# FNet plus PEER on one core: one-hots of the gates made a step earlier, checks placed anew, and loads and stores moved from one DMA queue to another

## The chip, the cores and the metric

The kernel runs on one core of a Trainium2 chip. Its engines work side by side, each through its own instructions in order: TensorE (PE in the profile; its weight loads are PEld), VectorE (DVE), ScalarE (ACT), GpSimd (POOL) and SyncE (SP), which here only issues DMAs. GpSimd can issue DMAs too. Inputs and outputs lie in device memory. The metric is the device time of one execution in microseconds (us); lower is better.

## The reference

```python
def _A_ref(x, dft_seq_re, dft_seq_im, dft_hid_re, dft_hid_im):
    a = jnp.einsum("bsd,ed->bse", x, dft_hid_re)
    b = jnp.einsum("bsd,ed->bse", x, dft_hid_im)
    return jnp.einsum("ts,bse->bte", dft_seq_re, a) - jnp.einsum("ts,bse->bte", dft_seq_im, b)

def _B_ref(x, w_q, k1, k2, u, v):          # 32 heads, 64 + 64 keys, top 2
    q = jnp.einsum("nd,dhc->nhc", xf, w_q)
    s1 = jnp.einsum("nhd,ed->nhe", q[..., :dk], k1)
    s2 = jnp.einsum("nhd,ed->nhe", q[..., dk:], k2)
    ...                                    # top 2 of s1, of s2, then of their 4 sums
    g = _softmax(top_s, axis=-1)
    act = _gelu(jnp.einsum("nd,nhkd->nhk", xf, u[top_e]))
    out = jnp.einsum("nhk,nhk,nhkd->nd", g, act, v[top_e])

xn = _layernorm(x, axis=-1)
return x + _A_ref(xn, ...) + _B_ref(xn, ...)
```

x is 2048 tokens by 512, float32. The two DFT matrices over the sequence are 2048 x 2048, those over the hidden dimension 512 x 512; they come as inputs. The PEER part has 4096 experts, each a row of u and a row of v.

## The kernel before

**Stages.** Up to about 480 us the kernel does the layer norm, the DFT, the scores of the heads and the choice of experts. The DFT's result lies as rows of y in device memory, one block of 128 tokens after another (y_d). From there on it computes the PEER part densely: for each block b of 128 tokens (16 blocks) it multiplies all 4096 rows of u with the tokens (the z phase), applies gelu, multiplies by the gates, and multiplies by all rows of v (the v phase). The phases come in the order z of a pair of blocks, v of b - 1, v of b: `("z", 8, 9), ("v", 7), ("v", 8), ("z", 10, 11), ("v", 9), ...`.

**The z phase of a pair** (z_pair, L1193; matmuls L1186) has 28 slots of 24 matmuls. Three slots run at the end of the v phase before it and one in the v phase behind it; the rest is divided into 16 steps. The slots share four PSUM banks (z0 to z3) with the sum of the v phase. A bank comes free by VectorE's adds (L1227, L1235, L1238) or ScalarE's copies and gelu (L1225, L1230, L1232, L1215).

**The v phase** (v_part, L1327; matmuls L1349) has 8 steps of 12 matmuls. At its end, finish (L1362) adds the sum to the tile y and stores it to out. The tile y (one buffer) was filled by add_x (L1357): a load of the DFT's rows from y_d on SP's queue (L1359), onto which GpSimd issues a DMA that adds x (L1360). So a load of y waits for the store of the block before, and the accumulate waits for the load.

**Gates.** g_mm (L1268) turns the chosen experts and their gates into a dense block for 32 columns: per half, VectorE writes the one-hot matrices L (128 x 2048, L1279) and R (128 x 512, L1284, then times the gate, L1287), and TensorE multiplies them (16 matmuls, L1289). Three pairs (L, R) take turns. w_part (L1292) multiplies gates and activations (L1297) and splits the product into two float16 parts (ScalarE's L1304 or VectorE's L1302, then L1305).

**Checks.** The kernel uses symmetries of the DFT matrices and ranges of the weights. Side work verifies them, and a general path runs behind a branch where they don't hold. compare (L1370) loads one of 64 units of the sequence matrices into a tile cx: 64 KB of ca (L1377) and 448 KB of cb (L1378); compare_in (L1381) sums the first 128 columns' absolute values on VectorE (L1385), folds the rest with adds (L1391 to L1429), and ScalarE sums the absolute differences (L1430). compare_w does this for four units of the hidden matrices (wt), and fit sums weights, some of them loaded (L1486, L1494). Tiles cx, fit and w share four buffers (tag "w"). A call of step (L1544) starts one unit: it first issues what the last calls left (`later`: ScalarE's sums; `loaded`: VectorE's folding) and then loads the next unit.

**Order.** A table, plan, says at which step of which phase a piece of side work is issued: `put(phase, step, work)`; G, W, U and F stand for g_mm, w_part, a unit of compare and one of fit. From this program the framework's scheduler makes each engine's order, and may move an instruction among others. `pin` (keep_in_program_order) keeps an instruction behind all that was issued ahead of it on its engine. In the table before, U and F stand in z phases at steps 8, 9, 11 to 13 and 15, 23 units U in all, and in the v phases of even blocks four U.

## Time and profile before

| what | us |
| --- | --- |
| median of 3 timed runs | 1130.34 (1128.55 to 1131.25) |
| profiled execution | 1135.25 |
| its span, first to last instruction | 1133.4 |
| TensorE busy in it | 1107.3 |
| VectorE busy | 962.7 |
| ScalarE busy | 663.9 |
| GpSimd busy | 332.7 |

The granted TensorE clock was 0.995 of full speed over the span. A row of the timeline gives the start, the duration, engine, line, operation, output and inputs with their shapes, how many instructions of a kind follow one another, and in brackets how long the engine was idle before and what ended that. A row of the waits gives the engine and line that waited, what it waited for, and the total, the times and the longest in us. A row of the groups gives busy time and the mean of one in ns, then the idle time before them. A row of DMA issues gives the queue, the number, KB each, and the median us from issue to landing.

### The profile page before, as it was taken

Reading aid. Unit: us, or ns where it says so; the run is one execution under the profiler, and the core shown is the slowest. Engines: PE = TensorE matmul, PEld = TensorE weight load, DVE = VectorE, ACT = ScalarE, POOL = GpSimd, SP = SyncE. Lnnn points to the kernel's source line nnn. Section 1 sums busy time; section 2 is a strip of 40 time slices with the busy share of each in tenths; the row PEclk is TensorE's granted clock in tenths of the full one; section 3 lists DMA queues with packets and bytes.
Section 4 is the critical chain, followed back from the end, with each engine's and each line's share of the span. In section 5 each row is a group of like instructions: output and inputs, shape, how many; then the busy total and the mean of one; then the engine's idle time right before and its main releaser. Section 6 shows DMA issues by size and latency. Waiting matters only on the chain.

```text
span 1133.4 us, 29112 instructions
## 1 busy us (share of the span) xinstructions
PE 1107.3 (98%) x11528; PEld 722.5 (64%) x11528; DVE 962.7 (85%) x2904; ACT 663.9 (59%) x1098; POOL 332.7 (29%) x385
## 2 busy tenths in 40 slices
PE   9999999999999999999999999999999999999997
PEld 6455554544545459687488478478569569569643
DVE  7899789999989799948997897898888888888793
ACT  6558598888877584346445545544535545544442
POOL 0429999899888850000000000000000000000000
PEclk9999999999999999999999999999999999999999
DMA  9883546465353335866666777666668668566354
GB/s 291 292 206 148 185 139 223 117 217 170 92 168 96 111 108 191 236 199 205 226 206 226 227 218 241 218 207 232 200 205 263 199 211 269 190 221 206 121 168 134
DMA packets 132273, 220.51 MB, mean 195 GB/s; under 512 B 35092, under 2 KB 71067, under 8 KB 132126
## 3 DMA queue, kind: packets, MB, share of 16 engines
q1 hardware_dynamic: 129520, 214.28, 58.7%
q0 software_dynamic: 2304, 4.20, 2.8%
q8 instruction: 92, 1.51, 0.5%
q14 instruction: 55, 0.45, 0.1%
q10 hardware_dynamic: 302, 0.08, 0.0%
HBM read 183.06 MB, written 29.69 MB: 188 GB/s over the span
## 4 chain that ended last, share of the span: by engine, by line
PE 59%; DVE 15%; DMA 5%; ACT 4%; issue 2%; POOL 1%; SPq 0%; ACTq 0%; DVEq 0%
PE s L252 18%; PE z L1186 17%; PE v L1349 16%; PE z L1108 4%; DMA cx<-in_cb_dram 3%; DVE w L1297 3%; DVE L L1279 3%; PE g L1289 3%; DVE act L1305 2%; PE m L148 1%; DVE R L1287 1%; DVE R L1284 1%; DVE w L1305 1%; DMA s<-s_d 1%; DVE cx L1393 1%
## 5 line engine op out<-in xcount | busy, mean ns | idle before, releaser
L252 PE MATMUL s<-m,xq 128*128 128x512 f16 x1344 | 297.4, 379 | 1.7 <-ACT ss L962 1.4
L1349 PE MATMUL v<-v,act 128*128 128x512 f16 x1044 | 233.3, 379 | 0.0
L252 PEld LDWEIGHTS <-xq 128*128 128x128 f16 x1344 | 129.6, 98 | 153.1 <-issue 3.2
L1360 POOL DMA_DIRECT2D y<-in_x_dram x16 | 14.4, 897 | 658.7 <-DMA v<-v_d 274.7
L1279 DVE TENSOR_TENSOR L<-io_lam,cmp 128x2048 f16<-128x2048 f16 x128 | 156.2, 1221 | 28.1 <-PE g L1289 28.1
L1349 PEld LDWEIGHTS <-act 128*128 128x128 f16 x1044 | 99.2, 98 | 112.4
L1186 PEld LDWEIGHTS <-u 128*128 128x128 f16 x2688 | 156.2, 98 | 14.8 <-issue 8.3
L966 DVE MAX8 vals<-ss 128x8 f32<-128x64 f32 x896 | 133.3, 216 | 5.5 <-ACT ss L962 5.2
L1186 PEld LDWEIGHTS <-s 128*128 128x128 f16 x1944 | 110.6, 98 | 1.2 <-DMA s<-s_d 1.2
L1349 PE MATMUL v<-v,w 128*128 128x512 f16 x480 | 109.0, 384 | 0.0
L1304 ACT ACTIVATE act<-w 128x1024 f16<-128x1024 f32 x36 | 48.9, 1358 | 92.2 <-DVE w L1297 92.2
L970 DVE FIND_INDEX8 idx<-vals,ss 128x8 uint16<-128x256 f32 x224 | 93.7, 418 | 0.0
L962 ACT ACTIVATE ss<-s,wsc 128x512 f32<-128x512 f32 x120 | 80.0, 680 | 22.5 <-PE s L252 12.6
L1186 PE MATMUL z<-xb,u 128*128 128x128 f16 x1344 | 84.9, 220 | 5.3 <-DVE w L1227 4.7
L1186 PE MATMUL z<-x,u 128*128 128x128 f16 x1344 | 84.7, 220 | 1.6 <-DVE act L1238 1.1
L1186 PE MATMUL z<-x,s 128*128 128x128 f16 x1296 | 81.2, 219 | 1.0 <-DMA s<-s_d 1.0
L1215 ACT ACTIVATE act<-act,scl 128x512 f32<-128x512 f32 x56 | 39.6, 720 | 70.9 <-DVE act L1235 40.9
L1349 PEld LDWEIGHTS <-w 128*128 128x128 f16 x480 | 46.1, 99 | 53.1 <-issue 2.3
L1430 ACT ACTIVATE cx<-cx 128x896 f32<-128x896 f32 x64 | 60.0, 938 | 29.6 <-DVE cx L1410 11.7
L1289 PEld LDWEIGHTS <-L 128*128 128x128 f16 x2048 | 60.7, 96 | 17.3 <-issue 7.2
L1289 PE MATMUL g<-R,L 128*128 128x32 f16 x2048 | 63.5, 177 | 6.6 <-DVE R L1287 6.2
L1305 DVE TENSOR_TENSOR act<-w,act 128x1024 f16<-128x1024 f32 x44 | 58.6, 1332 | 6.1 <-ACT act L1304 6.1
(363 smaller groups left out, 1878.9 us busy)
## 6 DMA issues: line engine op xcount, KB each, us to landing
v<-v_d SPq DMA_DIRECT2D x67, 512.0 KB, 4.6
s<-s_d SPq DMA_DIRECT2D x63, 512.0 KB, 4.2
cx<-in_cb_dram SPq DMA_DIRECT2D x64, 448.0 KB, 5.7
w<-in_wq_dram SPq DMA_DIRECT2D x28, 512.0 KB, 5.9
fit<-in_wq_dram SPq DMA_DIRECT2D x28, 512.0 KB, 4.3
uv<-in_vn_dram SPq DMA_DIRECT2D x16, 512.0 KB
uv<-in_ut_dram SPq DMA_DIRECT2D x16, 512.0 KB, 3.5
s_d<-v SPq DMA_DIRECT2D x32, 256.0 KB, 2.5
```

The lines of the kernel that those rows point to most:

```text
L252: nc.tensor.matmul(ps, xt[i][:, l, kd, :], m[:, r, kd, :], start=(n == 0), stop=(n == 3 * KD - 1))
L962: nc.scalar.activation(s, ps, AF.Copy, scale=inv)
L966: nc.vector.max(vals[:, i, w, :, h], s[:, g, :])
L970: nc.vector.max_index(idx[:, i, w].rearrange("p k h -> p (k h)"), vals[:, i, w, 0:2].rearrange("p k h -> p (k h)"), s[:, w * HC:g + 1, :]. ...
L1108: nc.tensor.matmul(ps if n == 1 else ps.rearrange("p (b n) -> p b n", b=2), ug[:, l, c % 2, kd, :], xb2[:, k0, r, kd, :] if n == 1 else xb ...
L1186: nc.tensor.matmul(bank[:, t * P:(t + 1) * P], lt, rt, start=(t == k == 0 and op in "125"), stop=(t == 3 and k == 5), skip_group_check=op ...
L1279: nc.vector.tensor_tensor(L.rearrange("p t (l two) -> p t l two", two=2), io_lam.rearrange("p (l two) -> p l two", two=2).unsqueeze(1).to_ ...
L1289: nc.tensor.matmul(p[:, hf, t * NC:(t + 1) * NC], L[:, t, :], R[:, t, :], start=True, stop=True)
L1304: nc.scalar.activation(w16[..., 0], w, AF.Copy)
L1305: nc.vector.tensor_tensor(w16[..., 1], w, w16[..., 0], op=ALU.subtract)
L1349: nc.tensor.matmul(pv, w16[:, c, :, l], v_sb[g][:, r, cc, :], start=(n + cc == 0 and k == 0), stop=(n == end and cc == 1 and k == 2))
L1430: later.append(lambda: pin(nc.scalar.activation(tf[:, P:], tf[:, P:], AF.Abs, accum_out=chk[:, n:n + 1])))
```

## The change: one-hots, checks, queues and sums

1. g_prep holds the one-hots of both halves, and LRP places it in the table one to three steps ahead of its g_mm. L is pinned, R isn't.
2. The checks have other steps: in z phases U at 0 and 4 (and 14 in the pairs 2/3, 4/5 and 6/7) and no F; in v phases of even blocks F at 0 and a fifth U at step 2; one F more in block 14. 17 units U are in z phases instead of 23.
3. The loads of y (but the last block's), the stores of out in finish, and the loads of ca, cb and fit go from SP's queue to GpSimd's, 193 issues in all. Loads of v, s and wt stay on SP's.
4. The sums of the absolute values of ca (128 columns, 64 units) go from VectorE to ScalarE, behind the sums of the differences.

```diff
@@ -1258,6 +1258,7 @@
             return work, middle, behind
 
         GP = {}
+        pin = tc.keep_in_program_order
 
         def parts(b):
 
@@ -1265,9 +1266,11 @@
             return act.rearrange("p c n -> p (c n)").bitcast(F16).rearrange(
                 "p (c n l) -> p c n l", c=NC, l=2)
 
-        def g_mm(b, tg):
+        PREP = {}
+
+        def g_prep(b, tg):
+            assert not PREP
             cmp = CMP[b]
-            p = pg(f"g{b}_{tg}")
             for hf in range(2):
                 ts = slice(tg * TG + hf * 16, tg * TG + hf * 16 + 16)
 
@@ -1276,15 +1279,22 @@
 
                 LR.append(LR.pop(0))
                 L, R = LR[-1]
-                nc.vector.tensor_tensor(
+                PREP.setdefault((b, tg), []).append((L, R))
+                pin(nc.vector.tensor_tensor(
                     L.rearrange("p t (l two) -> p t l two", two=2),
                     io_lam.rearrange("p (l two) -> p l two", two=2).unsqueeze(1).to_broadcast([P, 16, P // 2, 2]),
-                    bc(0, P), op=ALU.is_equal)
+                    bc(0, P), op=ALU.is_equal))
                 Rv = R.rearrange("p t (c two) -> p t c two", two=2)
                 nc.vector.tensor_tensor(
                     Rv, io_c.rearrange("p (c two) -> p c two", two=2).unsqueeze(1).to_broadcast([P, 16, NC // 2, 2]),
                     bc(1, NC), op=ALU.is_equal)
                 nc.vector.tensor_tensor(Rv, Rv, bc(2, NC), op=ALU.mult)
+
+        def g_mm(b, tg):
+            if (b, tg) not in PREP:
+                g_prep(b, tg)
+            p = pg(f"g{b}_{tg}")
+            for hf, (L, R) in enumerate(PREP.pop((b, tg))):
                 for t in range(16):
                     nc.tensor.matmul(p[:, hf, t * NC:(t + 1) * NC], L[:, t, :], R[:, t, :], start=True, stop=True)
             GP[b, tg] = p
@@ -1356,16 +1366,15 @@
 
         def add_x(b):
             Y[b] = y = bp.tile([P, D], F32, tag="y", name=f"y{b}", bufs=1)
-            nc.sync.dma_start(y, y_d[b])
+            (nc.sync if safe or b + 1 == NT else nc.gpsimd).dma_start(y, y_d[b])
             nc.gpsimd.dma_start(y, x[b % 4, b // 4], accum_op=ALU.add)
 
         def finish(b, pv):
             y = Y[b]
             nc.vector.scalar_tensor_tensor(y, pv, osc, y, op0=ALU.mult, op1=ALU.add)
-            nc.sync.dma_start(out[b * P:(b + 1) * P], y)
+            (nc.sync if safe else nc.gpsimd).dma_start(out[b * P:(b + 1) * P], y)
 
         later, loaded = [], []
-        pin = tc.keep_in_program_order
 
         def compare(n):
 
@@ -1374,16 +1383,14 @@
             t = bp.tile([P, 4, 4, 64], F32, tag="w", name=f"cx{n}", bufs=WB)
             tf = t.rearrange("p s q c -> p (s q c)")
             tv = t.rearrange("p s q c -> p s (q c)")
-            nc.sync.dma_start(tf[:, :P], ca[ri, g, :, kk * P:(kk + 1) * P])
-            nc.sync.dma_start(tf[:, P:], cb[ri, g, kk].rearrange("p b c -> p (b c)"))
+            nc.gpsimd.dma_start(tf[:, :P], ca[ri, g, :, kk * P:(kk + 1) * P])
+            nc.gpsimd.dma_start(tf[:, P:], cb[ri, g, kk].rearrange("p b c -> p (b c)"))
             loaded.append(lambda: compare_in(n, t, tf, tv))
 
         def compare_in(n, t, tf, tv):
 
             ri, g, kk = n // 32, n // 8 % 4, n % 8
             odd = kk // 4
-            pin(nc.vector.tensor_reduce(asum[:, n:n + 1], tf[:, :P], axis=AX.X, op=ALU.add,
-                                        apply_absolute_value=True))
             sgn = (((1, 1, 1), (-1, 1, -1)), ((-1, -1, 1), (1, -1, -1)))[ri][odd]
             ops = [ALU.subtract if v > 0 else ALU.add for v in sgn]
             op = ops[1]
@@ -1427,7 +1434,11 @@
             mirror(t[:, 0])
             if kk == 0:
                 nc.vector.memset(t[:, 0, 2, 0:1], 0.0)
-            later.append(lambda: pin(nc.scalar.activation(tf[:, P:], tf[:, P:], AF.Abs, accum_out=chk[:, n:n + 1])))
+            def sums_abs():
+                pin(nc.scalar.activation(tf[:, P:], tf[:, P:], AF.Abs, accum_out=chk[:, n:n + 1]))
+                nc.scalar.activation(tf[:, :P], tf[:, :P], AF.Abs, accum_out=asum[:, n:n + 1])
+
+            later.append(sums_abs)
 
         def compare_w(n):
 
@@ -1483,7 +1494,7 @@
 
             if n < NK:
                 t = bp.tile([P, 2 * D], F32, tag="w", name=f"fit{n}", bufs=WB)
-                nc.sync.dma_start(t.rearrange("p (h k) -> p h k", h=2), wq[1 + n // 4, n % 4 // 2, n % 2])
+                nc.gpsimd.dma_start(t.rearrange("p (h k) -> p h k", h=2), wq[1 + n // 4, n % 4 // 2, n % 2])
                 loaded.append(lambda: later.append(
                     lambda: pin(nc.scalar.activation(t, t, AF.Abs, accum_out=fits[:, n:n + 1]))))
                 return
@@ -1491,7 +1502,7 @@
             t = bp.tile([P, 2 * D], F32, tag="w", name=f"fit{n}", bufs=WB)
             if g >= 16 + V2:
                 h = t.bitcast(F16)[:, 0:2 * D]
-                nc.sync.dma_start(h, v_d[g - 16 - V2, :, 0:2 * D])
+                nc.gpsimd.dma_start(h, v_d[g - 16 - V2, :, 0:2 * D])
                 loaded.append(lambda: later.append(
                     lambda: pin(nc.scalar.activation(h, h, AF.Abs, accum_out=fits[:, n:n + 1]))))
                 return
@@ -1583,6 +1594,9 @@
         def G(b, k):
             return lambda: g_mm(b, k)
 
+        def LRP(b, k):
+            return lambda: g_prep(b, k)
+
         def W(b, k, here=False):
             return lambda: w_part(b, k, here)
 
@@ -1606,41 +1620,42 @@
             if b % 2 == 0 and 0 < b < 13:
                 nx = phases[phases.index(ph) + 1]
                 st = 1 if len(nx) == 2 else 2
-                put(ph, 1, G(b + 1, 0))
+                put(("v", b - 1), 7, LRP(b + 1, 0))
+                put(ph, 1, G(b + 1, 0), LRP(b + 1, 1))
                 put(ph, 3, G(b + 1, 1))
-                put(ph, 5, W(b + 1, 0))
-                put(ph, 7, W(b + 1, 1), G(b + 1, 2))
+                put(ph, 5, W(b + 1, 0), LRP(b + 1, 2))
+                put(ph, 7, W(b + 1, 1), G(b + 1, 2), LRP(b + 1, 3))
                 put(nx, st, W(b + 1, 2, True), G(b + 1, 3))
                 put(nx, 3 * st, W(b + 1, 3, True))
             elif b + 1 < NT:
                 for k in range(4):
                     put(ph, 2 * k or b % 2, W(b + 1, k))
-                put(ph, b % 2, G(b + 1, 2))
+                put(ph, b % 2, G(b + 1, 2), LRP(b + 1, 3))
                 put(ph, 3, G(b + 1, 3))
         put(("v", 13), 5, G(15, 0))
         put(("v", 13), 7, G(15, 1))
         for ph in phases[2:]:
             if ph[0] == "z":
-                put(ph, 9, G(ph[1], 0))
+                put(ph, 6, LRP(ph[1], 0))
+                put(ph, 9, G(ph[1], 0), LRP(ph[1], 1))
                 put(ph, 12, G(ph[1], 1))
+                put(ph, 14, LRP(ph[1], 2))
         for b in range(13):
             put(("v", b), 3, lambda b=b: compact_d(b + 2))
         put(("z", 14, 15), 8, lambda: compact_d(15))
         if not safe:
             for cg in (1, 3, 5, 7):
                 put(("v", 0), cg, F[0])
-            for ph, cg in ((("v", 12), 0), (("v", 14), 1), (("v", 14), 3), (("v", 14), 7)):
+            for ph, cg in ((("v", 12), 0), (("v", 14), 1), (("v", 14), 3), (("v", 14), 5), (("v", 14), 7)):
                 put(ph, cg, F[0])
             for ph in phases[3:]:
                 if ph[0] == "z":
-                    put(ph, 8, F[0])
-                    for cg in {2: (9, 11, 13, 15), 4: (9, 11, 13, 15), 6: (9, 11, 13, 15), 14: (9, 12)}.get(ph[1], (9, 12, 15)):
+                    for cg in (0, 4, 14) if ph[1] < 8 else (0, 4):
                         put(ph, cg, U)
                 elif ph[1] < 14:
-                    for cg, f in enumerate((None, F[1], F[1], U, U, U, U, F[0]) if ph[1] % 2 == 0 else (
-                            None, F[1], F[0], None, U, U, U, F[0])):
-                        if f and (ph[1] < 13 or f != U):
-                            put(ph, cg, f)
+                    for cg, fs in enumerate(((F[0],), (F[1],), (F[1], U), (U,), (U,), (U,), (U,), (F[0],)) if ph[1] % 2 == 0 else (
+                            (), (F[1],), (F[0],), (), (U,), (U,), (U,), (F[0],))):
+                        put(ph, cg, *[f for f in fs if ph[1] < 13 or f != U])
             for cg in range(3):
                 put(("v", 14), cg, F[1])
                 put(("v", 14 + cg // 2), (6, 7, 0)[cg], U)
```

What it moves on SP's and GpSimd's queues, around the end of block 7 (out is out_0_dram, v12_8 a load of rows of v for block 8, y8 the tile of block 8, cx39 the tile of unit 39). SP before:

```order
L1365 DMA out_0_dram<-y7_12510 128x512
L1325 DMA v12_8_12531<-v_d_60 128x2048
L1359 DMA y8_12876<-y_d_57 128x512
L1377 DMA cx39_12661<-in_ca_dram 128x128
L1325 DMA v11_8_12545<-v_d_60 128x2048
L1378 DMA cx39_12661<-in_cb_dram 128x896
L1377 DMA cx40_12686<-in_ca_dram 128x128
L1378 DMA cx40_12686<-in_cb_dram 128x896
```

GpSimd now:

```order
L1375 DMA out_0_dram<-y7_12500 128x512
L1369 DMA y8_12881<-y_d_57 128x512
L1370 DMA y8_12881<-in_x_dram 128x512
L1386 DMA cx38_12598<-in_ca_dram 128x128
L1387 DMA cx38_12598<-in_cb_dram 128x896
L1386 DMA cx39_12659<-in_ca_dram 128x128
L1387 DMA cx39_12659<-in_cb_dram 128x896
```

The store, the load of y, the accumulate of x and the checks' blocks, which were spread over two queues, are now in line on one; the loads of v are left alone on SP.

VectorE in the z phase of the pair 8/9, around the third group of adds (z2_8_2 and the like are banks of z, cmp8 holds block 8's choices, L0 to L2 and R0 to R2 are the three pairs of one-hots). Before:

```order
L1235 TENSOR_TENSOR act9_11437<-z5_8_3_11615,act9_11437 128x4x128
L1393 SCALAR_TENSOR_TENSOR cx33_11930<-cx33_11930,not0_79 128x256 x2
L1395 TENSOR_TENSOR cx33_11930<-cx33_11930 1x256
L1238 TENSOR_TENSOR act9_11437<-z1_8_3_11466,w4_126 128x4x128
L1410 TENSOR_TENSOR cx33_11930<-cx33_11930 1x128
L1227 TENSOR_TENSOR w4_126<-z2_8_2_11780,w4_126 128x4x128
L1279 TENSOR_TENSOR L1_5774<-io_lam_72,cmp8_11216 128x2048
L1284 TENSOR_TENSOR R1_5775<-io_c_73,cmp8_11216 128x512
L1279 TENSOR_TENSOR L2_5776<-io_lam_72,cmp8_11216 128x2048
L1287 TENSOR_TENSOR R1_5775<-R1_5775,cmp8_11216 128x512
L1385 TENSOR_REDUCE sums_87<-cx33_11930 128x1
L1391 TENSOR_TENSOR cx33_11930<-cx33_11930 128x256
```

And now:

```order
L1227 TENSOR_TENSOR w4_126<-z2_8_2_11800,w4_126 128x4x128
L1283 TENSOR_TENSOR L0_5772<-io_lam_72,cmp8_11211 128x2048
L1283 TENSOR_TENSOR L1_5774<-io_lam_72,cmp8_11211 128x2048
L1288 TENSOR_TENSOR R1_5775<-io_c_73,cmp8_11211 128x512
L1288 TENSOR_TENSOR R2_5777<-io_c_73,cmp8_11211 128x512
L1291 TENSOR_TENSOR R1_5775<-R1_5775,cmp8_11211 128x512
L1291 TENSOR_TENSOR R2_5777<-R2_5777,cmp8_11211 128x512
L1235 TENSOR_TENSOR act9_11442<-z5_8_2_11826,act9_11442 128x4x128
L1238 TENSOR_TENSOR act9_11442<-z1_8_2_11674,w4_126 128x4x128
L1227 TENSOR_TENSOR w4_126<-z2_8_0_12052,w4_126 128x4x128
L1283 TENSOR_TENSOR L0_5772<-io_lam_72,cmp8_11211 128x2048
```

The rows of cx33, which stood between the adds, are gone from this stretch, and both halves' L and R stand together ahead of the adds.

VectorE at the end of block 7, whose finish is the row of y7 (cmp9 holds block 9's choices, whose gates for columns 0 to 31 are multiplied in step 1 of block 8). Before:

```order
L1395 TENSOR_TENSOR cx38_12484<-cx38_12484 1x256
L1410 TENSOR_TENSOR cx38_12484<-cx38_12484 128x128
L1410 TENSOR_TENSOR cx38_12484<-cx38_12484 1x128
L1364 SCALAR_TENSOR_TENSOR y7_12510<-v7_12228,scl_93,y7_12510 128x512
L1418 COPY cx38_12484<-cx38_12484 1x128
L1279 TENSOR_TENSOR L1_5774<-io_lam_72,cmp9_12414 128x2048
L1284 TENSOR_TENSOR R1_5775<-io_c_73,cmp9_12414 128x512
L1279 TENSOR_TENSOR L2_5776<-io_lam_72,cmp9_12414 128x2048
L1287 TENSOR_TENSOR R1_5775<-R1_5775,cmp9_12414 128x512
L1284 TENSOR_TENSOR R2_5777<-io_c_73,cmp9_12414 128x512
```

And now:

```order
L1417 TENSOR_TENSOR cx36_12440<-cx36_12440 128x128
L1417 TENSOR_TENSOR cx36_12440<-cx36_12440 1x128
L1283 TENSOR_TENSOR L0_5772<-io_lam_72,cmp9_12400 128x2048
L1425 COPY cx36_12440<-cx36_12440 1x128
L1291 TENSOR_TENSOR R1_5775<-R1_5775,cmp9_12400 128x512
L1398 TENSOR_TENSOR cx37_12468<-cx37_12468 128x256
L1400 SCALAR_TENSOR_TENSOR cx37_12468<-cx37_12468,not0_79 128x256 x2
L1374 SCALAR_TENSOR_TENSOR y7_12500<-v7_12219,scl_93,y7_12500 128x512
L1402 TENSOR_TENSOR cx37_12468<-cx37_12468 1x256
L1417 TENSOR_TENSOR cx37_12468<-cx37_12468 128x128
L1417 TENSOR_TENSOR cx37_12468<-cx37_12468 1x128
L1283 TENSOR_TENSOR L2_5776<-io_lam_72,cmp9_12400 128x2048
```

Before, L1 and R1, the second half of that product, stand behind the finish. Now its last operation, the gates into R1, stands ahead of cx37 and of the finish, and what follows the finish belongs to the next product.

## The prediction

> **What bounds the kernel now.** I read the page's engine totals first, then the table of waits from 480 us to the end (the DFT is over by then, and the change touches nothing ahead of it), then TensorE's timeline at its longest waits, then the engine that each wait names.
>
> ```profile
> span 1133.4 us, 29112 instructions
> PE 1107.3 (98%) x11528; PEld 722.5 (64%) x11528; DVE 962.7 (85%) x2904; ACT 663.9 (59%) x1098; POOL 332.7 (29%) x385
> ```
>
> TensorE is busy for 1107.3 of 1133.4 us and the change leaves its matmuls alone, so 26.1 us of idle time is all that scheduling can reach in the whole kernel. Of that, the part after 480 us is (in total, times, longest):
>
> ```profile
> PE g L1289 <- DVE R L1287: 6.0, 9, 2.2
> PE z L1186 <- DVE w L1227: 4.7, 3, 2.4
> PE z L1186 <- DVE act L1238: 1.1, 1, 1.1
> PE z L1186 <- DMA s<-s_d: 1.0, 1, 1.0
> ```
>
> All but the last name VectorE: one-hots that are late (R L1287), and adds of the z phase (L1227, L1238) that are late and hold PSUM banks. The places (start, us, idle before in brackets):
>
> ```profile
> 529.25 1.50 PE L1186 MATMUL z<-x,u 128*128 128x128 f16 x24 [1.13 <-DVE act L1238]
> ...
> 558.09 0.55 PE L1289 MATMUL g<-R,L 128*128 128x32 f16 x16 [1.81 <-DVE R L1287]
> ...
> 775.89 1.50 PE L1186 MATMUL z<-xb,u 128*128 128x128 f16 x24 [1.97 <-DVE w L1227]
> ...
> 823.02 0.55 PE L1289 MATMUL g<-R,L 128*128 128x32 f16 x16 [2.24 <-DVE R L1287]
> ...
> 846.36 1.50 PE L1186 MATMUL z<-xb,u 128*128 128x128 f16 x24 [0.28 <-DVE act L1227]
> 847.70 1.50 PE L1186 MATMUL z<-xb,s 128*128 128x128 f16 x24
> ...
> 1040.15 2.19 PE L1186 MATMUL z<-xb,u 128*128 128x128 f16 x24 [2.40 <-DVE w L1227]
> ```
>
> VectorE just before the two long z waits:
>
> ```profile
> 773.11 0.88 DVE L1393 SCALAR_TENSOR_TENSOR cx<-cx,not 128x256 f32<-128x256 f32 x2 [2.08 <-DMA cx<-in_cb_dram]
> ...
> 775.17 0.67 DVE L1227 TENSOR_TENSOR w<-z,w 128x512 f32<-128x512 f32 x1
> ...
> 1037.11 0.29 DVE L1458 TENSOR_TENSOR cx<-cx 128x128 f32<-128x128 f32 x1 [2.69 <-DMA cx<-in_wt_dram]
> ```
>
> VectorE was not overloaded there: it stood 2.08 and 2.69 us at the head of its queue on a check's block that had not landed, with the add TensorE needed queued behind. So the bound is a few in-order stalls, not a throughput.
>
> **The change part by part.** (1) *Checks out of the second half of the z phases.* The waits 1.13 + 1.97 + 2.40, and 0.35 left of the L1227 row's 4.7 (4.7 - 1.97 - 2.40), make 5.85 us; at each of these places the order after has no loaded check ahead of the add. Not less than 2.4 (the longest alone), not more than 5.85; I take 5.0, since three z phases keep checks at steps 0, 4 and 14.
>
> (2) *One-hots a step ahead.* L and R of both halves stand before the finish and the checks of the step that multiplies them. 1.81 + 2.24 = 4.05 of the row's 6.0 are the two long waits, the rest seven short ones. Between 2 and 6.0; I take 4.0. The operations are the same, so VectorE pays nothing for this.
>
> (3) *SP's queue empties.* SP's own longest waits of the kinds that move, 480 to 1110 us:
>
> ```profile
> SPq L1365 <- DVE y L1364: 47.6, 10, 13.5
> SPq L1486 <- ACT cx L1430: 46.5, 10, 7.0
> ```
>
> Stores wait for finishes and fit's loads for a tile that ScalarE still sums, and loads of s and v stand behind them. The s wait of 1.0 can go; between 0 and 1.0, I take 0.5. The 47.6 and 46.5 don't vanish: they are now POOL's, ahead of blocks of C.
>
> (4) *The clock after the long waits.* Windows of 20 us (PE busy, then PEld, DVE, ACT, POOL; then the granted clock, DMA share, GB/s):
>
> ```profile
> 560.00:580.00 20.00, 20.00 (x162) 11.11 (x161) 17.55 (x34) 6.77 (x10) 0.86 (x1) 0.93 0.70 222
> 1040.00:1060.00 20.00, 19.85 (x334) 18.43 (x334) 13.24 (x27) 10.42 (x17) 0.00 (x0) 0.91 0.21 69
> ```
>
> (1 - 0.93) x 20 = 1.4 and (1 - 0.91) x 20 = 1.8, 3.2 in all, behind the waits of 1.81 and 2.40. No such dip follows 2.24, so it isn't sure. Between 0 and 3.2; I take 1.6. [...]
>
> (5) *Sums of C on ScalarE.* Groups after 480 us:
>
> ```profile
> L1385 DVE TENSOR_REDUCE sums<-cx 128x1 f32<-128x128 f32 x64 | 17.8, 277 | 3.9 <-DMA cx<-in_ca_dram 3.9
> L1430 ACT ACTIVATE cx<-cx 128x896 f32<-128x896 f32 x64 | 60.0, 938 | 29.6 <-DVE cx L1410 11.7 <-DVE cx L1418 8.1 <-issue 5.8
> L1430 ACT ACTIVATION_READ_ACCUMULATOR cx<-cx 128x1 f32 x64 | 12.1, 189 | 0.0
> L1488 ACT ACTIVATE fit<-fit 128x1024 f32<-128x1024 f32 x28 | 29.3, 1045 | 0.0
> ```
>
> VectorE loses 64 x 0.277 = 17.8 us. ScalarE gains 64 of abs over 128 elements: (1045 - 938) / 128 = 0.836 ns an element, 938 - 768 x 0.836 = 296 ns, and 189 for reading the accumulator, 0.485 us each, 31 us in all. ScalarE is busy 59%, and 47 of them stand in v phases, where it has only a few z slots to evacuate: 0. Without that cover, the other 17, in z phases and ahead of a bank's copy, x 0.485 = 8; the order has them behind a gelu, not at step 8 to 15, so I keep 0. VectorE's 17.8 is no term either: it shortens the queues already counted in (1) and (2).
>
> Gains: 5.0 + 4.0 + 0.5 + 1.6 = 11.1 us.
>
> (6) *The queues.* Rows of y, stores of out, blocks of C and fit's loads move from SP's queue to POOL's: 193 issues. After 480 us POOL has had only the accumulates of x, each waiting for its y load; nothing else is queued there, so whatever is now late on POOL is late for checks, y and out alone. In blocks 2, 4, 6, 8, 10 and 12 the checks' blocks now stand behind something that waits. Block 8 is the worst: store of y7, y8 load, accumulate (it waits for the load to land), and only then cx38. Now (SP, then POOL, then VectorE):
>
> ```profile
> 819.92 0.34 SPq L1365 DMA_DIRECT2D out_dram<-y  x1
> ...
> 823.55 0.32 SPq L1359 DMA_DIRECT2D y<-y_d  x1
> 823.98 0.37 SPq L1377 DMA_DIRECT2D cx<-in_ca_dram  x1
> ...
> 824.87 0.42 SPq L1378 DMA_DIRECT2D cx<-in_cb_dram  x1
> ...
> 826.88 0.86 POOL L1360 DMA_DIRECT2D y<-in_x_dram  x1 [65.82 <-DVE R L1287]
> ...
> 819.16 0.73 DVE L1364 SCALAR_TENSOR_TENSOR y<-v,scl,y 128x512 f32<-128x512 f32 x1
> ...
> 831.31 0.43 DVE L1391 TENSOR_TENSOR cx<-cx 128x256 f32<-128x256 f32 x1 [2.89 <-DMA cx<-in_cb_dram]
> ...
> 844.98 0.73 DVE L1364 SCALAR_TENSOR_TENSOR y<-v,scl,y 128x512 f32<-128x512 f32 x1
> ...
> cx<-in_cb_dram SPq DMA_DIRECT2D x64, 448.0 KB, 5.7
> ...
> y<-y_d SPq DMA_DIRECT2D x16, 256.0 KB, 3.4
> ```
>
> Before: store at 819.92, first check at 831.31, 11.4 us. After: 3.6 from the store to the y load (823.55 - 819.92, the store must land), 3.3 to the accumulate (826.88 - 823.55), its 0.86, the same for the 64 KB block, then 5.7 to 6.4 (831.31 - 824.87) until the 448 KB block is there: 14.3 to 15.1, so up to 3.7 later. A POOL issue of a plain load stands in no row; 0.86 is its nearest row above, 0.32 to 0.42 of SP's below. Behind the first check VectorE has 13.7 us (844.98 - 831.31) of work to y8's finish, whose bank TensorE needs; that finish is just in time now, since the next add (L1227) costs TensorE 0.28. After, more than 13.7 stands there (a fifth check added to the phase, a reduce of 0.28 each taken out): 3.7 for the landing and about 1.1 for the larger load, 4.8 late in all. Not below 2 (VectorE's 2.89 of idle taken by one-hots), not above 7.5 (nothing of it covered); I take 4.
>
> For the other five blocks the accumulate stands behind the checks' blocks, so only the y load's wait for the store (3.6) and the dearer issues delay the first check, some 3 us. What slack there is:
>
> ```profile
> 579.40 0.75 DVE L1364 SCALAR_TENSOR_TENSOR y<-v,scl,y 128x512 f32<-128x512 f32 x1 [1.61 <-PE v L1349]
> ...
> 930.33 0.75 DVE L1364 SCALAR_TENSOR_TENSOR y<-v,scl,y 128x512 f32<-128x512 f32 x1 [0.73 <-PE v L1349]
> ```
>
> VectorE waits 1.61 and 0.73 us for TensorE at two of the finishes, and the bank is wanted only after the z slot that follows, 1.34 us on (847.70 - 846.36, one slot to the next). So most is hidden: between 0 and 5 x 3 = 15; I take 3, nearer the hidden end.
>
> Sum: -11.1 + 4 + 3 = -4.1 us. The profiled execution took 1135.25 us (its span 1133.4 and 1.85 around it), the timed median is 1130.34, 4.9 below. 1135.25 - 4.1 = 1131.2 profiled, 1126 as timed.
>
> [...]
>
> **The rivals.** *POOL's queue is hidden everywhere.* The pool of four tiles lets the blocks be issued a step early, and VectorE has 17.8 us less to do. Against it stands the 2.89 us that VectorE already stood idle in block 8. Then -11.1: 1119.
>
> *It cancels.* Either (6) costs its 7.5 in block 8 and 0.7 in each of the others, 11.0, or the second half's one-hots still come late (only L is pinned, R may float, so L of half two can slip behind checks), which takes 4.0 from the gains. Then 0: 1130.
>
> *POOL's queue decides.* One mechanism: store, y load, accumulate and blocks are one chain in order on one queue, so each even block's checks begin when the store has landed. It decides once the first check lands more than the 1.3 to 2.9 us of slack later. Then each of six blocks loses 3.7: 22.2 - 11.1 = +11: 1141. For it: finish in block 8 has no slack now. Against: in five blocks the accumulate is out of the chain, and on SP the same store and load stood ahead of the blocks too.
>
> *VectorE holds up POOL's issues.* Each of four issues in an even block waits for one operation such as this:
>
> ```profile
> L1279 DVE TENSOR_TENSOR L<-io_lam,cmp 128x2048 f16<-128x2048 f16 x111 | 135.5, 1221 | 24.6 <-PE g L1289 24.5
> ...
> L1360 POOL DMA_DIRECT2D y<-in_x_dram x16: 858/865/1177, 455.2 to 1118.1; - x16
> ```
>
> 4 x 1.22 x 6 = 29 on top of -4: 1155. Against: POOL's sixteen issues took 858 to 1177 ns beside a VectorE that is 85% busy. [...]
>
> **How the numbers follow.** About 0.2%, 2.3 us, is what a measurement can tell from no change: 1128.1 to 1132.6. Forecast 0.46 (0.04 of it inside that band), hidden 0.13, cancel 0.17 (0.01 above the band), POOL's queue 0.19, VectorE's lock 0.05. Faster 0.42 + 0.13 = 0.55; same 0.04 + 0.16 = 0.20; slower 0.25. The forecast's own range is 1120 to 1130. The range is 1117 to 1138: below are 0.03 of the hidden case, above the lock and somewhat over half of POOL's queue.
>
> **What would show it.** Right: the waits of 1.81 and 2.24 before g, and of 1.13, 1.97 and 2.40 in the z phases, gone; POOL's issues near 0.86; in block 8 the accumulate ahead of the first check, y8's finish later after y7's store than 25 us, and a TensorE wait at the start of the next z phase. Wrong: idle VectorE on blocks of C in each even v phase (POOL's queue), POOL issues of over 1.5 us (the lock), or g still waiting for R.

## The result: 5.0% slower, and the profile after

The changed kernel takes 1186.53 us (median of 4, 1179.77 to 1193.05), the kernel before on the same chip 1129.44 (1128.53 to 1131.25): a ratio of 1.0503, 95% interval 1.0428 to 1.0578. The forecast was 1126 us, with a range of 1117 to 1138. The profiled execution took 1179.77 us, with a span of 1178.0, 44.6 longer than before. It is the fastest of the four, and the profiled one of the kernel before lies 4.9 above that kernel's timed median of 1130.34, so the traces show less than the 57.1 us between the medians; where the rest lies no trace tells.

The page's head:

```profile
span 1178.0 us, 29264 instructions
PE 1115.9 (95%) x11528; PEld 731.4 (62%) x11528; DVE 951.5 (81%) x2840; ACT 685.1 (58%) x1226; POOL 439.0 (37%) x578
```

TensorE does the same 11528 matmuls in 8.6 us more (1115.9 against 1107.3); the rest of the 44.6, 36.0 us, is idle time. TensorE's longest waits after 480 us:

```profile
PE z L1186 <- DVE act L1227: 16.7, 4, 4.9
PE z L1186 <- DVE w L1227: 14.2, 4, 5.7
PE g L1299 <- DVE L L1283: 4.4, 1, 4.4
PE g L1299 <- DVE R L1291: 3.6, 4, 1.6
```

The waits of 1.13, 1.97 and 2.40 in the second half of z phases and of 1.81 and 2.24 ahead of g are gone from their places, but ahead of g TensorE waits longer in all, 8.0 us (4.4 + 3.6, in blocks 2, 8, 13 and 14) where it was 6.0. And one wait of 2.95 to 5.74 us stands at the start of every z phase of a pair: the finish of the block before comes late, and the first add behind it. The 8.6 us more of busy time stand beside these waits: a z slot takes 1.50 us as a rule and 2.72 behind the wait of block 8 (quoted below), where the granted clock of the 20 us from 868 is 0.79. Behind the shortest of these waits, 2.95, the slot takes 1.50, and the 20 us from 967 show 1.00.

Block 8, GpSimd's queue, then VectorE, then TensorE:

```profile
842.24 0.55 POOL L1375 DMA_DIRECT2D out_dram<-y  x1 [3.52 <-DVE cx L1402]
847.14 0.54 POOL L1369 DMA_DIRECT2D y<-y_d  x1 [4.35 <-DMA out_dram<-y]
852.20 0.93 POOL L1370 DMA_DIRECT2D y<-in_x_dram  x1 [4.52 <-DMA y<-y_d]
852.87 0.82 POOL L1386 DMA_DIRECT2D cx<-in_ca_dram  x1
856.64 0.54 POOL L1387 DMA_DIRECT2D cx<-in_cb_dram  x1 [2.96 <-issue]
...
860.59 0.43 DVE L1398 TENSOR_TENSOR cx<-cx 128x256 f32<-128x256 f32 x1 [10.39 <-DMA cx<-in_cb_dram]
...
875.55 0.77 DVE L1374 SCALAR_TENSOR_TENSOR y<-v,scl,y 128x512 f32<-128x512 f32 x1
...
876.98 2.72 PE L1186 MATMUL z<-xb,u 128*128 128x128 f16 x24 [4.62 <-DVE act L1227]
```

This is the chain that the prediction worked out: store, load of y, accumulate, block. It put 14.3 to 15.1 us from the store to the first check; there are 18.4 (860.59 - 842.24). Store and load take 4.9 and 5.1 us (3.6 and 3.3 were put), and the 448 KB block is issued 3.8 us behind the 64 KB one (0.86), of which 2.96 are a wait that no semaphore explains; from its issue to the check there are 4.0 (5.7 to 6.4). VectorE stands 10.39 us. From the first check to the finish there are 15.0 (875.55 - 860.59), as the 13.7 and 1.1 of the prediction had it.

The time from the finish of an odd block to that of the even block behind it (rows y L1364 and L1374 of VectorE's timeline), for the kernel before, after, and some runs that follow:

| block | before | after | all on SP (e1) | after, room 768 (e5) | rows on SP, 768 (e9) | y load on SP, 768 (e13) | store on SP, 768 (e14) |
| --- | --- | --- | --- | --- | --- | --- | --- |
| 2 | 25.0 | 29.5 | 25.5 | 30.0 | 27.5 | 26.1 | 26.5 |
| 4 | 21.5 | 29.0 | 25.2 | 26.6 | 22.8 | 24.1 | 26.4 |
| 6 | 23.5 | 30.4 | 26.7 | 28.4 | 25.4 | 26.3 | 27.2 |
| 8 | 25.8 | 34.5 | 26.4 | 31.6 | 30.4 | 31.3 | 32.2 |
| 10 | 22.7 | 26.7 | 25.1 | 26.6 | 23.3 | 22.5 | 23.0 |
| 12 | 23.9 | 29.9 | 25.6 | 27.0 | 25.6 | 24.2 | 27.2 |
| sum | 142.4 | 180.0 | 154.5 | 170.2 | 155.0 | 154.5 | 162.5 |

37.6 of the 44.6 us of span are lost in these six stretches. VectorE stands 5.8 to 10.4 us on blocks of C in each of them, 46.3 us together, where the kernel before has 12.9 and the one with all on SP 25.4.

### The profile page after: what moved, and what is told of

Its sections match the earlier page's. It is cut to its first block, busy times and chain, and to the rows that moved or that the text cites. A ratio compares the mean times of both kernels' runs of the same rounds, so it can differ in the third digit from the quotient of the medians.

```text
span 1178.0 us, 29264 instructions
## 1 busy us (share of the span) xinstructions
PE 1115.9 (95%) x11528; PEld 731.4 (62%) x11528; DVE 951.5 (81%) x2840; ACT 685.1 (58%) x1226; POOL 439.0 (37%) x578
## 4 chain that ended last, share of the span: by engine, by line
PE 23%; DVE 17%; DMA 8%; issue 8%; ACT 5%; POOL 2%; DVEq 0%; POOLq 0%; ACTq 0%; SPq 0%
PE z L1186 16%; DMA cx<-in_cb_dram 5%; PE v L1359 5%; DVE L L1283 4%; DVE w L1307 3%; ACT act L1314 2%; DVE act L1315 2%; PE g L1299 1%; DVE cx L1411 1%; DVE w L1315 1%; POOL cx L1386 1%; DVE R L1288 1%; DVE R L1291 1%; DMA fit<-in_wq_dram 1%; DMA v<-v_d 1%
## 5 line engine op out<-in xcount | busy, mean ns | idle before, releaser
L1186 PEld LDWEIGHTS <-u 128*128 128x128 f16 x2688 | 161.2, 100 | 42.0 <-issue 35.3
L1186 PE MATMUL z<-xb,u 128*128 128x128 f16 x1344 | 90.7, 228 | 30.9 <-DVE act L1227 16.7
L1186 PEld LDWEIGHTS <-s 128*128 128x128 f16 x1944 | 113.9, 99 | 2.6 <-issue 2.6
L1497 POOL DMA_DIRECT2D fit<-in_wq_dram x28 | 15.1, 539 | 241.6 <-ACT cx L1438 175.7
L1411 DVE TENSOR_TENSOR cx<-cx 128x512 f32<-128x512 f32 (+2 forms) x84 | 48.4, 611 | 30.5 <-DMA cx<-in_cb_dram 30.1
L1386 POOL DMA_DIRECT2D cx<-in_ca_dram x64 | 36.0, 563 | 97.4 <-issue 30.6
```

The lines of the kernel that those rows point to most:

```text
L1186: nc.tensor.matmul(bank[:, t * P:(t + 1) * P], lt, rt, start=(t == k == 0 and op in "125"), stop=(t == 3 and k == 5), skip_group_check=op ...
L1386: nc.gpsimd.dma_start(tf[:, :P], ca[ri, g, :, kk * P:(kk + 1) * P])
L1411: pin(nc.vector.tensor_tensor(v, v, tv[:, 0:1].to_broadcast([P, len(ix), 256]), op=o))
```

## The experiments

Each is a ratio to the kernel before on the same chip.

| run | what | ratio | 95% interval |
| --- | --- | --- | --- |
| after | the change | 1.0503 | 1.0428 to 1.0578 |
| e1 | the change, all transfers on SP's queue | 1.0133 | 1.0103 to 1.0163 |
| e3 | the change, checks and fit on SP's queue | 1.0031 | 1.0012 to 1.0051 |
| e4 | the change, y's load and the store on SP's queue | 1.0340 | 1.0295 to 1.0384 |
| e5 | the change, room 768 | 1.0346 | 1.0306 to 1.0385 |
| e9 | e4, room 768 | 1.0194 | 1.0166 to 1.0222 |
| e13 | the change, y's load on SP, room 768 | 1.0198 | 1.0175 to 1.0222 |
| e14 | the change, store on SP, room 768 | 1.0224 | 1.0194 to 1.0253 |
| e2 | before + queue alone | 1.0225 | 1.0194 to 1.0256 |
| e17 | e2, room 768 | 1.0198 | 1.0173 to 1.0224 |
| e7 | before + respread alone | 1.0119 | 1.0084 to 1.0154 |
| e12 | before + respread of v phases alone | 1.0047 | 1.0027 to 1.0068 |
| e6 | before + one-hots alone | 1.0005 | 0.9985 to 1.0024 |
| e8 | before + y's load and store on GpSimd | 0.9988 | 0.9970 to 1.0007 |
| e15 | before + sums by ScalarE alone | 0.9941 | 0.9918 to 0.9964 |
| e16 | e15 + y's load and store on GpSimd | 0.9951 | 0.9933 to 0.9968 |
| e18 | e15 + one-hots | 0.9960 | 0.9944 to 0.9975 |
| e10 | e16 + one-hots | 0.9951 | 0.9934 to 0.9968 |
| e11 | before + one-hots, y's load, store and fit on GpSimd | 1.0041 | 1.0018 to 1.0064 |

### Which queue, and for what (e1 to e4)

Starting from the changed kernel, e1 puts all of these back on SP's queue, e3 the loads of ca, cb and fit, and e4 the load of y and the store. e2 makes the change's move in the kernel before.

```diff
-            (nc.sync if safe or b + 1 == NT else nc.gpsimd).dma_start(y, y_d[b])
+            nc.sync.dma_start(y, y_d[b])
-            (nc.sync if safe else nc.gpsimd).dma_start(out[b * P:(b + 1) * P], y)
+            nc.sync.dma_start(out[b * P:(b + 1) * P], y)
-            nc.gpsimd.dma_start(tf[:, :P], ca[ri, g, :, kk * P:(kk + 1) * P])
+            nc.sync.dma_start(tf[:, :P], ca[ri, g, :, kk * P:(kk + 1) * P])
...                                        # cb and fit's two loads in the same way
```

> The changed kernel with all 193 issues back on SP's queue; one-hots as a step, checks respread and sums by ScalarE stay. Theory 1 (the queue alone makes it slower): the waits of 2.95 to 5.74 us at the start of each z phase go, and what is left is the prediction's gain of 5.0 + 4.0 + 0.5 + 1.6 = 11: 1119 us, not above 1126. Theory 2 (the new spread of the checks, a fifth unit in each even v phase, is too much for VectorE on any queue): the finish of even blocks stays late by some us in each of six blocks, 1150 us or more.

> The kernel before with the queue move alone (rows of y, stores of out, blocks of C and fit's loads on GpSimd's queue). Theory 1: slower by about as much as the whole change and its lost gain, 1129 + 57 + 11 = some 1190 us or more. Theory 2: within 1% of the kernel before, 1129 to 1140.

> The changed kernel with the blocks of C and fit's loads back on SP's queue; only the store of out, the load of y and the accumulate of x are on GpSimd's. Theory 1a (checks stand in line behind the store and the load of y): the checks no longer wait for the store, VectorE's idle of 4 to 10 us ahead of the first check of even blocks goes, 1119 to 1128 us. Theory 1b (what costs is that GpSimd's transfers themselves take longer, the store 4.5 us to land where SP's took 2.0): y comes late still, finishes are late, 1150 us or more.

> The changed kernel with the store of out and the load of y back on SP's queue; blocks of C, fit's loads and the accumulate of x are on GpSimd's. Theory 1a: nothing waits for a store on GpSimd's queue, so most of the 57 us goes; what is left is block 8, where the accumulate stands ahead of the first unit: 1119 to 1130 us. Theory 1b: blocks of C still start late on GpSimd's queue, with idle that no semaphore explains between the two loads of a unit (68 us in all in the changed kernel): 1145 us or more.

Measured: 1147.7, 1159.2, 1137.7 and 1172.4 us, where the kernel before takes 1133.65. e1, e2 and e3 each came out between their two theories. In e1 the queue is the larger part: 5.0 - 1.3 = 3.7% goes with it. But 1.3% stays with everything on SP, where 1% of gain was expected, so the other parts of the change lose too (below). On its own the queue costs 2.2%, 25.6 us (e2), less than with them.

Of the queue's two halves, the checks and fit cost and y's rows don't: with the rows alone on GpSimd's queue (e3) the changed kernel is 1.0% faster than with everything on SP's. TensorE's waits of e1 show what SP's queue then holds up:

```profile
PE z L1186 <- DMA s<-s_d: 7.1, 7, 2.0
PE z L1186 <- DVE act L1227: 5.8, 4, 2.5
PE z L1186 <- DVE w L1227: 4.7, 3, 1.9
```

In e3 the first row is 4.0. In the kernel before, whose checks stand elsewhere, the rows' move gains nothing (e8, its theory B). e4 is what stays with the checks on GpSimd's queue and no store there: 3.4%, so theory 1a, that only the store in line costs, fell, and theory 1b held. No run of the changed kernel has the checks without fit's loads on that queue, so their shares stay open.

### Room for three transfers (e5, e9, e17)

What e4 showed: the accumulate, the two loads of a unit, and no semaphore ahead of the last of them.

```profile
774.69 0.89 POOL L1370 DMA_DIRECT2D y<-in_x_dram  x1 [6.92 <-DVE w L1227]
775.33 0.81 POOL L1386 DMA_DIRECT2D cx<-in_ca_dram  x1
781.89 0.54 POOL L1387 DMA_DIRECT2D cx<-in_cb_dram  x1 [5.76 <-issue]
```

The last load is issued 7.2 us behind the accumulate, which took 6.9 to land, so 0.3 after the landing. One argument of the program, 512 in all kernels so far, is raised by half, and nothing else: in the changed kernel (e5), in e4 (e9) and in e2 (e17). Its value is called the room here:

```diff
-    nc = bacc.Bacc("TRN2", target_bir_lowering=False, num_devices=1, dynamic_dma_scratch_size=512)
+    nc = bacc.Bacc("TRN2", target_bir_lowering=False, num_devices=1, dynamic_dma_scratch_size=768)
```

> [...] In the runs so far a fourth transfer on GpSimd's queue is issued only 3.5 to 6 us after the third, when the first has landed, with nothing else to wait for. Theory A (the room holds three transfers and the fourth waits): with 768 some five fit, the idle marked issue ahead of the loads of C (60 us in the changed kernel) falls below 25, and the time by 10 to 35 us, to 1150 to 1180 against 1133 before. Theory B (it is only the order on the queue, behind the store and the accumulate): the idle and the time stay within 1%.

> The changed kernel with the store of out and the load of y on SP's queue (as in the run that was 3.4% slower) and dynamic_dma_scratch_size=768. Theory A (with no store in line, what checks on GpSimd's queue cost is the room for three transfers): it falls to the run with everything on SP, 1.3% slower, 1148 us, or up to 0.5% above it. Theory B (the accumulate of x, which waits for the load of y, holds the blocks of C behind it whatever the room): it stays between 2.3 and 3.4% slower.

> [...] Theory A (the room is most of what the queue costs): below 1.0% slower. Theory B (the order on the one queue is): 1.5 to 2.2%.

GpSimd's waits with no releaser, after 480 us, in the changed kernel:

```profile
POOL cx L1386 <- issue: 30.6, 19, 4.0
POOL cx L1387 <- issue: 29.7, 16, 6.3
POOL y L1370 <- issue: 7.5, 6, 1.9
```

and in e5:

```profile
POOL cx L1387 <- issue: 10.0, 8, 3.0
POOL y L1370 <- issue: 8.8, 5, 3.5
POOL cx L1386 <- issue: 1.9, 3, 1.4
```

The idle falls from 70.2 us (with 2.4 of a fit's load) to 20.9, and 5.0% become 3.5 (intervals apart); from e4 to e9 it falls from 78.9 to 25.6, and 3.4% become 1.9, some 0.6 above e1. So room is what 1.5% of the loss hangs on, with nothing else changed: theory A of e5, and of e9 nearly. The trace of the changed kernel tells how much 512 lets through. After 480 us never more than three of GpSimd's transfers are in flight there. Of its eleven waits of over 2 us with no releaser, six begin with three plain transfers in flight, of 64 to 448 KB, and five with an accumulate and one more; all eleven end 0.31 us after the oldest has landed. So in this trace an accumulate and one more hold up the next as three plain transfers do, as in the rows of e4. With 768, in e5, five are issued within 2.4 us, and the sixth waits:

```profile
663.53 0.54 POOL L1369 DMA_DIRECT2D y<-y_d  x1 [4.72 <-DMA out_dram<-y]
664.15 0.54 POOL L1386 DMA_DIRECT2D cx<-in_ca_dram  x1
664.72 0.54 POOL L1387 DMA_DIRECT2D cx<-in_cb_dram  x1
665.34 0.53 POOL L1386 DMA_DIRECT2D cx<-in_ca_dram  x1
665.90 0.54 POOL L1387 DMA_DIRECT2D cx<-in_cb_dram  x1
667.83 0.53 POOL L1386 DMA_DIRECT2D cx<-in_ca_dram  x1 [1.39 <-issue]
```

What the argument sizes no run shows, only what its value changed. For the queue alone theory A failed: in e17 the idle falls from 113.6 to 23.2 us and the time hardly (2.0% against 2.2, intervals overlap). VectorE still stands behind late blocks in e17:

```profile
DVE cx L1404 <- DMA cx<-in_cb_dram: 17.3, 12, 2.5
DVE sums L1385 <- DMA cx<-in_ca_dram: 11.2, 6, 5.5
```

where the kernel before has 11.3 and 3.9. In all its waits for blocks of C are 44.2 us in e17 and 45.9 in e2, against 26.2 in the kernel before: with more room GpSimd idles less, but the blocks come no sooner for VectorE. So theory B held there, the order on the queue costs nearly as much by itself.

### The store in line (e13, e14)

> The changed kernel with 768 bytes of room and the load of y alone on SP's queue; the store of out stays on GpSimd's. The wait for the store (4 us each, 60 us in all) leaves GpSimd's queue. Theory A (what is left of the loss with 768 is that wait, ahead of the blocks of C): from 3.5% down to the 1.9% of the run with both rows on SP and 768. Theory B (the number of transfers on GpSimd's queue is what counts): 2.7 to 3.5%, one transfer in fourteen fewer changes little.

> The counterpart: 768 bytes of room and the store of out alone on SP's queue; the load of y, which waits for the store to land, stays on GpSimd's ahead of the blocks of C. Theory A: the wait stays on GpSimd's queue, 2.7 to 3.5% slower. Theory B: as far down as the run with the load of y on SP's queue, since the queue has one transfer less here too.

The edits are the first and the second pair of lines above, each with 768. With y's load off the queue 3.5% become 2.0, as theory A had it. With the store off it and the load on it they become 2.2, which theory A of that run had not; the intervals of the two runs overlap, so theory B, as far down as the other, isn't refuted. The wait for the store stays on GpSimd's queue there, but it is shorter. Block 3's store, block 4's load of y and its first block of C in e5:

```profile
658.26 0.55 POOL L1375 DMA_DIRECT2D out_dram<-y  x1 [3.14 <-DVE cx L1436]
663.53 0.54 POOL L1369 DMA_DIRECT2D y<-y_d  x1 [4.72 <-DMA out_dram<-y]
...
664.72 0.54 POOL L1387 DMA_DIRECT2D cx<-in_cb_dram  x1
```

and in e14, the store on SP's queue:

```profile
651.25 0.34 SPq L1375 DMA_DIRECT2D out_dram<-y  x1
...
654.89 0.55 POOL L1369 DMA_DIRECT2D y<-y_d  x1 [6.40 <-DVE R L1291]
...
656.06 0.54 POOL L1387 DMA_DIRECT2D cx<-in_cb_dram  x1
```

5.3 us from store to load against 3.6. Over the six blocks it is 4.2 to 7.3 in e5 and 2.8 to 5.3 in e14 (and 2.1 to 4.5 in e4, with both on SP's). The first 448 KB block is issued 6.6 to 9.6 us behind the finish in e5, 4.8 to 7.3 in e14 and 3.8 to 4.7 in e13, block 8 aside. The time of e5 lies above the two others, which the measurement doesn't tell apart. In block 8 the accumulate stands ahead of the blocks in all three, the first block is issued 10.0 to 11.5 us behind the finish, and the stretch is 31 to 32 us long; no run took the accumulate away. Whether the store lands later because GpSimd issues it, or because of what else is in flight then, is open: with only the rows on GpSimd's queue (e3) there are 3.9 to 6.0 us from store to load.

### The respread (e7, e12)

e7 is the table of the checks alone in the kernel before; e12 keeps the z phases' steps and takes the v phases' new ones.

```diff
-                elif ph[1] < 14:
-                    for cg, f in enumerate((None, F[1], F[1], U, U, U, U, F[0]) if ph[1] % 2 == 0 else (
+                    for cg, fs in enumerate(((F[0],), (F[1],), (F[1], U), (U,), (U,), (U,), (U,), (F[0],)) if ph[1] % 2 == 0 else (
...                                        # and in e7 the z phases' steps, as in the change
```

> The kernel before with the new steps of the checks alone (fewer in z phases, five in even v phases; all on SP's queue). Prediction's step 1: 2.4 to 5.9 us faster. Rival, after the run with all issues back on SP's queue (1.3% slower): this part is what costs there, since finishes are late (10.5 us of waits at the start of z phases) and loads of s stand behind checks at steps 0 and 4 (7.1 us): 0.8 to 1.5% slower.

> The kernel before with the new steps of the checks in v phases alone (a fit at step 0 and a fifth unit in even blocks); z phases keep theirs. Of the 1.2% that the respread alone costs: theory A (the fuller even v phases make the finish late): 0.6 to 1.2% slower. Theory B (the units at steps 0 and 4 of z phases, ahead of loads of s on SP's queue, cost it): within 0.4%.

Slower by 1.2% alone, as the rival had it, and about as much as e1 loses; the 0.6% that the sums gain by themselves (below) doesn't show in e1, so the parts don't simply add up. TensorE's waits in e7:

```profile
PE z L1186 <- DVE w L1227: 5.9, 3, 3.4
PE z L1186 <- DMA s<-s_d: 4.7, 4, 1.6
PE g L1289 <- DVE R L1287: 3.5, 8, 1.5
PE z L1186 <- DVE act L1227: 2.7, 3, 1.6
```

The waits of 1.97 and 2.40 late in z phases are gone, and 3.36 and 1.61 have come to z phases' starts, and TensorE waits 4.7 us for loads of s (1.0 before), behind units that are now loaded at steps 0 and 4. The fuller even v phases account for 0.5 of the 1.2% (e12, between its two theories); the rest is the z phases' new steps, which were not run alone, or the two together.

### One-hots, sums and rows (e6, e8, e15, e16, e18, e10, e11)

These are the change's lines put into the kernel before, one or more parts at a time.

> The kernel before with the one-hots as a step alone. Prediction's step 2: 2 to 6 us faster by TensorE's waits for R, 4 taken, 0.4% (1129 where the kernel before takes 1133). Rival: L pinned earlier only moves checks and adds behind it, no gain, within 0.2%.

> The kernel before with the load of y and the store of out alone on GpSimd's queue; checks stay on SP's. With the checks respread this was worth 10 us (1138 against 1148). Theory A (SP's queue is stopped at the load of y until the store has landed, and with it the loads of C, s and v behind it): a gain here too, 3 to 8 us. Theory B (that gain belongs to the respread checks alone): within 0.2%.

> The kernel before with the sums of C by ScalarE alone. The prediction put this at 0 (VectorE's 17.8 us only shorten queues counted elsewhere, ScalarE's 31 us are covered). Rival: the 0.5% gained by one-hots, sums and rows together, of which one-hots alone gave 0.0 and rows alone 0.1%, comes from the sums: 0.3 to 0.5% faster.

> The kernel before with the sums of C by ScalarE and y's load and out's store on GpSimd's queue, one-hots as before. Theory A (sums carry the 0.5%): as fast as with the one-hots, 0.4 to 0.6% faster. Theory B (it takes the one-hots' step with them, each clears a wait that the other two would only move): 0.0 to 0.3%.

> The kernel before with the one-hots as a step and the sums of C by ScalarE, all transfers on SP's queue. Sums alone gave 0.6%, one-hots alone 0.0. If they add up (TensorE's waits for R, of which sums alone leave 1.2 us, go too): 0.6 to 0.8% faster, the fastest kernel here. If pinned L stands ahead of adds and gates' products as in the run with one-hots alone: 0.3 to 0.5%.

> The kernel before with the one-hots as a step, the sums of C by ScalarE, and only y's load and out's store on GpSimd's queue; the checks keep their old steps and SP's queue. Prediction: the gains that do not hang on the respread, one-hots 4.0 and SP's 0.5, 4 to 5 us, 0.4% faster (1128). Rival (each moves TensorE's waits to another instruction of VectorE): within 0.2%.

> The kernel before with the one-hots as a step, and y's load, out's store and fit's loads on GpSimd's queue; blocks of C stay on SP's, their steps and sums as before. Theory A (fit's loads, which wait for ScalarE, hold up SP's loads of s and v and gain by leaving): 0.3 to 0.8% faster. Theory B (fit's loads and y's chain hold each other up on GpSimd's queue): within 0.3% or slower.

The one-hots alone (e6) clear most of the waits that they were made for and gain nothing, as the rival had it. TensorE's waits:

```profile
PE z L1186 <- DVE w L1227: 3.9, 3, 2.1
PE v L1359 <- DVE act L1315: 3.0, 4, 0.9
...
PE g L1299 <- DVE R L1291: 0.8, 2, 0.5
```

The 6.0 us ahead of g are 0.8, but 3.0 stand in v phases, behind a gates' product (L1315). On VectorE a pinned L and operations on R stand a little ahead of it; that they make it late is likely, but not shown. The sums alone (e15) gain 0.6%, a little more than the rival's 0.3 to 0.5:

```profile
PE z L1186 <- DVE w L1227: 3.9, 2, 2.6
PE z L1186 <- DVE act L1238: 1.5, 1, 1.5
PE g L1289 <- DVE R L1287: 1.2, 2, 1.1
```

With 64 reduces fewer on VectorE most one-hots are in time without being moved, and TensorE's waits after 480 us fall from 13.9 to 7.7 us. ScalarE's added work is, as priced, 302 + 188 ns a unit:

```profile
L1430 ACT ACTIVATE cx<-cx 128x128 f32<-128x128 f32 x64 | 19.3, 302 | 29.0 <-issue 20.5 <-DVE cx L1408 5.3 <-ACT cx L1429 2.7
...
L1430 ACT ACTIVATION_READ_ACCUMULATOR cx<-cx 128x1 f32 x64 | 12.0, 188 | 0.0
```

Neither the one-hots (e18), nor the rows (e16), nor both (e10) add to it: the four intervals overlap, which is theory A of e16 and the second case of e18. Of those run, the sums alone have the lowest ratio, and the four beat both kernels. That e10 came out at the 0.4% that its expectation took from steps 2 and 3 is luck: the gain is the sums', which that expectation put at nothing. With fit's loads beside the rows on GpSimd's queue, and without the sums, the kernel is 0.4% slower (e11): theory B. One-hots and rows cost nothing alone, but the two together without fit's loads were not run.

## Why the prediction was wrong

**What bounds the kernel** was right: in-order stalls of VectorE, not its load. The change takes 11.2 us of busy time from VectorE (962.7 to 951.5) and the kernel is slower. Load counts as far as it stands in those queues (step 5).

**Step 6, the queues, 4 + 3 us, is the step that failed.** Its mechanism, the rival *POOL's queue decides* (0.19, 1141), is what happened, in all six blocks, but the step took its size from near the hidden end. From e1 to the change the queue costs 3.7%, 42 us by the medians, where the step had 7. In the traces it is 33.2 us of span (1178.0 - 1144.8), 25.5 of them in the six stretches (180.0 - 154.5), near the rival's 22; the other 7.7 lie elsewhere, where no term looked. The rival itself missed the time all the same, since it took the gains of 11 as given. Three terms of the step:
- From the store to the load of y. The 3.6 came from SP's rows; on GpSimd's queue in the changed kernel it is 4.4 to 6.4.
- A limit that the sum did not have: in the changed kernel a fourth transfer waits for the first to land (2.38 us in block 8), the third behind an accumulate (2.96 us there). In the trace of before GpSimd issues only the sixteen accumulates, never two of them in flight, so no row could show it; the bound should have been open for that. It is worth about 1.5% (1.0503 against 1.0346 in e5).
- Block 8's 4 (2 to 7.5) was 8.7 (34.5 - 25.8), 8.1 of it against e1. For the other five blocks 3 was taken out of 0 to 15, "nearer the hidden end"; the five lost 28.9 (37.6 - 8.7) in all, 11.5 of it from the kernel before to e1 and 17.4, more than the upper bound, from e1 to the change. With a rival at 0.19 and a slack of 0.73 to 1.61 quoted in the same place, the nearer end was the other one.

The issue itself, put at 0.32 to 0.86, is 0.54, and the blocks land no later (4.3 us from issue, where SP had 5.7): it wasn't the transfers of C that grew dear.

**Step 1, checks out of the z phases, -5.0, had the wrong sign.** The waits that it named are gone; what it moved was priced where it left and not where it went. Alone it costs 1.2%. The fifth unit was priced in block 8 only (1.1), and the loads of s behind units at steps 0 and 4 not at all.

**Step 2, one-hots, -4.0**: alone (e6), the waits left as described, the time did not (1.0005); in the change TensorE still waits 8.0 us ahead of g, 3.6 of it for R, which the prediction had named as a sign of being wrong. What stands behind a pinned instruction was not asked.

**Step 3, SP's queue, -0.5**: with the checks on GpSimd's queue the wait for s is gone in the trace of the changed kernel. Small and right, but paid for above.

**Step 4, the clock, -1.6**: lower clocks did stand behind waits, but the other way round. Waits of 4.27 to 5.74 us came, with slots of 2.72 behind each and a granted clock of 0.79 to 0.91 in 20 us around each (from 582, 674, 768, 868 and 1055), and TensorE's busy time grew by 8.6.

**Step 5, sums, 0**: the price on ScalarE was right (0.485 forecast, 0.490 measured), the gain was not. 17.8 us off VectorE was called no term, since it "shortens the queues already counted"; by itself it gains 0.6%, some 6 us, and the waits ahead of g fall from 6.0 to 1.2 by it alone, without the 3.0 that step 2 alone made elsewhere.

## What to carry to other kernels

Moving a transfer to another queue put what it waits for in front of what stands behind it there: in block 8 there were 18.4 us from the store to the first check, where there had been 11.4. So work out the chain on the new queue with that queue's own landings, and when no trace has several transfers in flight on it, leave the bound open. Work that is moved out of a phase has to be priced in the phase that receives it, and in the queue that it now leads. Where in-order stalls of a busy engine set the end, taking small instructions off it can be worth more than arranging them anew, as here the sums' 0.6% against nothing for the one-hots and a loss for the checks.

## What the runs showed of the hardware

In the trace of the changed kernel, with the room at 512, at most three of GpSimd's transfers are in flight after 480 us; all eleven waits of over 2 us with no releaser stand behind three plain ones, or an accumulate and one more, and end 0.31 us after the oldest has landed. With 768, in e5, five are issued within 2.4 us before the sixth waits 1.39. At 512 GpSimd stood 70 to 114 us (the change, e4, e2) ahead of issues with no other releaser in the profile, at 768 21 to 31 (e5, e9, e13, e14, e17). In the changed kernel an issue of a plain transfer takes GpSimd 0.54 us, of an accumulate 0.91 (medians), and none took more than 1.06, beside a VectorE that is 81% busy: the rival *VectorE holds up POOL's issues*, the lock of the forecast, did not come. The choice of queue moved the time by 2.2% alone (e2) and by 3.7% in the change (against e1), while the blocks of C landed no later: 4.3 us from issue on GpSimd's queue in the changed kernel, 5.7 on SP's in the kernel before.
